# One square per score tile, or two half squares: splitting the square bank by bank

## The chip, the cores and the metric

The kernel runs on one core of one Trainium2 chip. The time is the device time of one execution in microseconds (us); medians are over all runs in the normal ("fast") state. The span of a profile leaves out the launch, so it is some 2 us shorter than the time. A trace is the profile of one execution. The engines are named as the profile names them: PE (matmuls), PEld (its weight loads), DVE, ACT, POOL (GpSimd) and SP (queue of transfers).

## The reference, cut to what matters

```python
# q, k, v: 8 batches, 12 heads, 448 positions, 64 wide
scores = scale * np.matmul(q, k.transpose(0, 1, 3, 2))
attn = np.maximum(scores, 0.0) ** 2 / S            # relu, then square
out = np.matmul(attn, v)
# then a two-layer network over 3584 tokens:
h = x @ w_in                                       # 768 -> 2048
g = np.maximum(h, 0.0) ** 2
return g @ w_out                                   # 2048 -> 768
```

The change touches one line of this: how the square in `attn` is cut into instructions.

## The kernel before

A unit is four heads of one batch. Its scores are made in tiles of two banks of PSUM, `sp[0]` and `sp[1]`, of up to 512 columns each. DVE or ACT takes the relu of each bank (from PSUM to `rel`, in fp32), and then **one** instruction on ACT or POOL squares both halves into `at` (or `comb`), which the value matmuls read:

```python
"rel": fixed(sb, "rel", 4, [P, 1024], FP32),
# ...
def square(op, sp, width, pool="at"):
    at, r = Buf(pool), Buf("rel")
    # ... rel() and dst() are views [128, 2, width] of the two buffers
    n = 2 * width
    first = [plan.add([
        dve(width, lambda e=e: nc.vector.tensor_scalar(
            out=rel()[:, e], in0=sp[e].tile[:, 0:width], ...)),        # relu and scale
        act(width, lambda e=e: nc.scalar.activation(
            out=rel()[:, e], in_=sp[e].tile[:, 0:width], func=AF.Relu, scale=SK))],
        [op], [sp[e], r], due=plan.now + 0.2) for e in range(2)]
    second = plan.add([
        act(n, lambda: nc.scalar.activation(out=dst(), in_=rel(), func=AF.Square)),
        ("POOL", 0.0018 * n + 0.05, 0.0018 * n + 0.08,
         lambda: nc.gpsimd.tensor_mul(dst(), rel(), rel()))],
        first, [r, at], due=plan.now + 4.0)
    return second, at
```

Nothing is emitted in the order of this text. `plan.add` records an operation with its alternatives (engine, price, duration), and a planner simulates the engines before the kernel is built, for 16 sets of rules (four patiences by four leads), and emits the order that ends first in its own model.

The first 21 score rounds (three units) are done in two parts: a first of 128 columns per round (`comb` tiles, 512 wide), and a later part of 320. They are "the start" below, 27 squares; the other 147 tiles are 448 wide per bank.

Of the kernel before, what the change touches and what calls it, by code (L numbers as in the profile page):

```python
# [12 lines left out]
FP32 = mybir.dt.float32  # L13
AF = mybir.ActivationFunctionType
ALU = mybir.AluOpType
# [274 lines left out]
def kernel(  # L290
# [9 lines left out]
    nc = tc.nc  # L300
# [7 lines left out]
    P = 128  # L308
# [9 lines left out]
    SK = 256.0  # L318
# [4 lines left out]
    sb = ctx.enter_context(tc.tile_pool(name="sb", bufs=1))  # L323
    psum = ctx.enter_context(tc.tile_pool(name="ps", bufs=1, space=bass.MemoryType.PSUM))

    def fixed(pool, name, n, shape, dt):
        return [pool.tile(shape, dt, name=f"{name}{i}", tag=f"{name}{i}") for i in range(n)]
# [13 lines left out]
        "rest": fixed(sb, "rest", 2, [P, NF, P], FP16),  # L341
        "comb": fixed(sb, "comb", 6, [P, NH, P], FP16),
        "part": fixed(sb, "part", 6, [P, HALF], FP32),
        "rel": fixed(sb, "rel", 4, [P, 1024], FP32),
        "mm": fixed(psum, "mm", 8, [P, 512], FP32),
    }
    plan = Plan(pools, {"PE": 5.0, "ACT": 0.7, "DVE": 1.2, "POOL": 1.4, "SP": 0.7})
    plan.cold = 6.6

    def act(n, emit):  # L350
        return "ACT", 0.09 + 0.00081 * n, 0.187 + 0.00081 * n, emit

    def dve(n, emit):
        return "DVE", 0.07 + 0.001045 * n, 0.149 + 0.001045 * n, emit
# [137 lines left out]
    def scores(rounds, bufs, cols, joint, at=None):  # L492
# [4 lines left out]
        def emit():  # L497
            for j, (n, t) in enumerate(rounds):
                qT, kT = qkt[n, "q"][1].tile, qkt[n, "k"][1].tile
                sp, c0 = bufs if joint else bufs[2 * j:2 * j + 2], j * w if joint else 0  # L500
                for e in range(2):
                    for f in range(2):
# [11 lines left out]
                       [y for x in turned for y in x[0]], bufs + [x[1] for x in turned],  # L514
                       "tile", at)

    def square(op, sp, width, pool="at"):
        at, r = Buf(pool), Buf("rel")
        flat = [2, width]

        def rel():
            return r.tile[:, 0:2 * width].rearrange("p (e c) -> p e c", e=2)

        def dst():
            t = at.tile
            if pool == "comb":
                t = t.rearrange("p f c -> p (f c)").rearrange("p (e c) -> p e c", e=2)
            return t[:, :, 0:width]

        n = 2 * width  # L530
        first = [plan.add([
            dve(width, lambda e=e: nc.vector.tensor_scalar(  # L532
                out=rel()[:, e], in0=sp[e].tile[:, 0:width], scalar1=0.0, scalar2=SK,
                op0=ALU.max, op1=ALU.mult)),
            act(width, lambda e=e: nc.scalar.activation(  # L535
                out=rel()[:, e], in_=sp[e].tile[:, 0:width], func=AF.Relu, scale=SK))],
            [op], [sp[e], r], due=plan.now + 0.2) for e in range(2)]
        second = plan.add([
            act(n, lambda: nc.scalar.activation(out=dst(), in_=rel(), func=AF.Square)),  # L539
            ("POOL", 0.0018 * n + 0.05, 0.0018 * n + 0.08,  # L540
             lambda: nc.gpsimd.tensor_mul(dst(), rel(), rel()))],  # L541
            first, [r, at], due=plan.now + 4.0)
        return second, at

    xts: dict = {}
    xt_ops: dict = {}
# [3 lines left out]
    def av(n, ts, cols=WHOLE, at=None):  # L550
        b, u = divmod(n, NU)
        x = xts.setdefault(b, Buf("xt"))
        w = cols.stop - cols.start
        first = cols == PARTS[0]
        joint = first and u > 0
        c0 = u * w if first else 0
        if ts[0] == 0:
            opened[n] = opened[n - 1] if joint else [Buf("mm"), Buf("mm")]
        banks = opened[n]
        used = [ats.pop((n, t)) for t in ts]  # L560

        def emit():
            vs = vst[n][1].tile
            for t, (_, buf, view) in zip(ts, used):
                a = view(buf.tile)
                for e in range(2):
                    for c in range(2):
                        f = c ^ e
                        r = slice(64 * c, 64 * c + 64)
                        nc.tensor.matmul(  # L570
                            banks[f].tile[64 * e:64 * e + 64, c0:c0 + w],
                            lhsT=vs[r, e ^ c, t * D:(t + 1) * D],
                            rhs=a[r, e, :],
                            start=(t == 0), stop=(t == TJ - 1), skip_group_check=True)

        before = av_ops.get(n, [])[-1:] + (av_ops[n - 1][-1:] if joint else [])
        op = plan.pe(max(0.1, 0.000437 * w) * len(ts), emit, [z[0] for z in used] + [vst[n][0]] + before,
                     [z[1] for z in used] + [vst[n][1]] + banks, "tile", at)
        av_ops.setdefault(n, []).append(op)
        if ts[-1] < TJ - 1 or (first and u < NU - 1):  # L580
            return op
        for f in range(2):
            def put(kind, f=f):
                def run():
                    dst, src = x.tile[:, 2 * u + f, cols], banks[f].tile[:, 0:w]
                    if joint:
                        dst = x.tile[:, f:NM:2, cols]
                        src = banks[f].tile[:, 0:NU * w].rearrange("p (u c) -> p u c", c=w)
                    if kind == "ACT":
                        nc.scalar.activation(out=dst, in_=src, func=AF.Copy, scale=CX)  # L590
                    else:
                        nc.vector.tensor_scalar_mul(dst, src, CX)
                return run

            n_el = NU * w if joint else w
            xt_ops.setdefault((b, cols.start), []).append(plan.add(
                [act(n_el, put("ACT")), dve(n_el, put("DVE"))], av_ops[n][-1:],
                [banks[f], x], due=plan.now + 0.2))
        return op
# [415 lines left out]
    def put(part, rs):  # L1015
        for r in rs:
            ats[r] = held.pop((part, *r))
        for n in sorted({n for n, _ in rs}):
            av(n, [t for m, t in rs if m == n], PARTS[part])
# [5 lines left out]
    def tile(part, rs, at=None):  # L1025
        cols = PARTS[part]
        w = cols.stop - cols.start
        sp = [Buf("mm"), Buf("mm")]
        op = scores(rs, sp, cols, True, at)
        second, at = square(op, sp, len(rs) * w, "at" if part else "comb")  # L1030
        for j, (n, t) in enumerate(rs):
            def view(tl, j=j, w=w, part=part):
                if not part:
                    tl = tl.rearrange("p f c -> p (f c)").rearrange("p (e c) -> p e c", e=2)
                return tl[:, :, j * w:(j + 1) * w]
            held[part, n, t] = second, at, view
# [19 lines left out]
    for z, one in enumerate(ORDER.split()):  # L1056
        at, n = 15.0 + 0.01 * z, int(one[1])
# [7 lines left out]
    for i in range(2, STREAM):  # L1065
# [3 lines left out]
        if i % TJ == 2 and i > TJ:  # L1069
            n = i // TJ - 1  # L1070
# [12 lines left out]
    for i in range(STREAM // 2, NB):  # L1083
# [19 lines left out]
        for n, t in rs:  # L1103
            sp = [Buf("mm"), Buf("mm")]
            op = scores([(n, t)], sp, WHOLE, False)
# [4 lines left out]
        for op, sp, n, t in todo:  # L1110
            second, at = square(op, sp, S)
            ats[n, t] = second, at, lambda tl: tl
        if i in avs:
            last, chain = chain, av(avs[i], list(range(TJ)))
            last.glue = chain
# [9 lines left out]
    for j in sorted(j for j in avs if j >= NB):  # L1125
        av(avs[j], list(range(TJ)))
# [35 lines left out]
```

## Time and profile before

| | before |
|---|---|
| median time (3 runs) | 383.08 us (382.96 to 383.53) |
| profiled span, granted clock | 382.0 us, 0.994 |
| busy PE / DVE / ACT / POOL | 371.8 / 268.5 / 272.0 / 191.0 us |
| squares on ACT / POOL | 110 / 64 |
| 4th first-layer group starts | 31.95 us |
| first group of the ordinary first layer starts | 35.89 us |
| PE busy between 57 and 88 us | 30.73 of 31 us |

The first layer for the three units of the start has a special form: four groups of six matmuls `mm<-w,xt`, each over one quarter of the first weight matrix. Then comes its ordinary form, `mm<-xt,w`. The profile lines themselves are in the prediction.

### The profile page before, as it was taken

How to read it: one execution, taken by the hardware profiler on the slowest of the kernel's cores; microseconds unless marked ns; L12 is line 12 of the kernel's file. 1: busy time of each engine (PE TensorE's matmuls, PEld its weight loads, DVE VectorE, ACT ScalarE, POOL GpSimd, SP SyncE). 2: the span in 40 equal slices, each digit the busy share in tenths (PEclk: the TensorE clock that was granted, in tenths of full speed). 3: DMA queues.
4: the chain of work that ended last, by engine and by line, in shares of the span. 5: the costliest groups of instructions: out<-in, count | busy, mean ns of one | idle time of the engine just before them, and what ended most of it. 6: DMA issues, size and time to landing. Idle time of an engine off the chain costs nothing.

```text
span 382.0 us, 8653 instructions
## 1 busy us (share of the span) xinstructions
PE 371.8 (97%) x3283; PEld 197.9 (52%) x3283; DVE 268.5 (70%) x464; ACT 272.0 (71%) x500; POOL 191.0 (50%) x184
## 2 busy tenths in 40 slices
PE   7799999999999999999999999999999999999995
PEld 3445565544465445544554555545555545555553
DVE  2976889687975677687996575885886768256731
ACT  4998999699877788687876786786794784244221
POOL 7987768383726665565564554664641333001000
PEclk9989999999999999999999999999999999999999
DMA  8999998987278966559369664674553002300243
GB/s 179 194 208 198 195 225 221 247 194 167 48 184 190 159 177 135 120 142 206 79 127 218 159 169 73 180 170 94 129 105 82 2 1 54 73 21 0 61 106 82
DMA packets 70216, 51.34 MB, mean 134 GB/s; under 512 B 36896, under 2 KB 70176, under 8 KB 70176
## 3 DMA queue, kind: packets, MB, share of 16 engines
q1 hardware_dynamic: 52384, 35.86, 38.2%
q0 software_dynamic: 16928, 14.09, 24.6%
q10 hardware_dynamic: 864, 0.85, 0.6%
q8 instruction: 25, 0.41, 0.4%
q14 instruction: 15, 0.12, 0.1%
HBM read 45.61 MB, written 11.01 MB: 148 GB/s over the span
## 4 chain that ended last, share of the span: by engine, by line
PE 92%; ACT 2%; DMA 2%; DVE 1%; POOL 1%; issue 1%; POOLq 0%; ACTq 0%
PE mm L632 38%; PE mm L846 31%; PE mm L505 10%; PE mm L570 8%; PE mm L781 3%; DMA g<-in_q_dram 2%; PE mm L681 2%; PE mm L444 1%; ACT comb L539 1%; DVE comb L825 1%; ACT rel L535 0%; POOL at L541 0%; DVE g L616 0%; ACT at L539 0%; PE mm L708 0%
## 5 line engine op out<-in xcount | busy, mean ns | idle before, releaser
L632 PE MATMUL mm<-xt,w 128*128 128x448 f16 (+1 forms) x768 | 149.0, 346 | 0.1
L541 POOL TENSOR_TENSOR at<-rel 128x896 f16<-128x896 f32 (+1 forms) x63 | 102.2, 1626 | 92.5 <-DVE rel L532 76.5
L616 DVE SCALAR_TENSOR_TENSOR g<-mm,g 128x448 f16<-128x448 f32 (+1 forms) x128 | 77.3, 605 | 50.4 <-ACT g L621 48.9
L632 PEld LDWEIGHTS <-w 128*128 128x128 f16 x768 | 72.3, 98 | 70.4 <-issue 11.7
L532 DVE TENSOR_SCALAR rel<-mm 128x448 f32<-128x448 f32 (+2 forms) x172 | 95.6, 596 | 15.7 <-PE mm L505 14.1
L621 ACT ACTIVATE g<-mm 128x448 f16<-128x448 f32 (+1 forms) x128 | 68.4, 539 | 47.2 <-PE mm L632 47.1
L539 ACT ACTIVATE at<-rel 128x896 f16<-128x896 f32 (+1 forms) x105 | 97.7, 948 | 1.1 <-DVE rel L532 0.6
L535 ACT ACTIVATE rel<-mm 128x448 f32<-128x448 f32 (+2 forms) x176 | 84.8, 550 | 2.9 <-PE mm L505 2.7
L846 PEld LDWEIGHTS <-comb 128*128 128x128 f16 x416 | 39.5, 98 | 30.3 <-issue 4.3
L765 ACT ACTIVATE part<-mm 128x384 f32<-128x384 f32 x45 | 22.3, 499 | 44.6 <-PE mm L846 42.3
L505 PE MATMUL mm<-qkt,qkt 64*64 64x448 f16 (+2 forms) x756 | 52.6, 340 | 1.4 <-DVE rel L532 0.3
L424 POOL CAST blk<-raw 128x896 f16<-128x896 f32 x36 | 36.5, 1024 | 23.4 <-DMA raw<-in_k_dram 11.7
L858 DVE SCALAR_TENSOR_TENSOR part<-mm,part 128x384 f32<-128x384 f32 x52 | 28.3, 554 | 24.9 <-ACT part L765 13.8
L846 PE MATMUL mm<-wt,comb 128*128 128x384 f16 x208 | 36.8, 327 | 0.2 <-DVE comb L825 0.2
L846 PE MATMUL mm<-w,comb 128*128 128x384 f16 x208 | 36.7, 327 | 0.0
L846 PEld LDWEIGHTS <-g 128*128 128x128 f16 x264 | 25.3, 98 | 19.1 <-issue 2.7
L570 PE MATMUL mm<-at,vs 64*64 64x448 f16 (+1 forms) x672 | 35.1, 344 | 0.0
L505 PEld LDWEIGHTS <-qkt 64*64 64x64 f16 x756 | 19.1, 106 | 26.2 <-issue 21.4
L474 POOL DMA_DIRECT2D vs<-in_v_dram x48 | 29.8, 631 | 4.2 <-DVE rel L532 2.0
L846 PE MATMUL mm<-w,g 128*128 128x384 f16 x176 | 31.1, 327 | 0.1
L570 PEld LDWEIGHTS <-vs 64*64 64x64 f16 x756 | 22.2, 108 | 14.7 <-issue 4.9
L747 POOL COPY rest<-g 128x1024 f16<-128x1024 f16 x8 | 8.8, 1103 | 40.6 <-DVE g L616 40.6
(61 smaller groups left out, 207.8 us busy)
## 6 DMA issues: line engine op xcount, KB each, us to landing
out_dram<-part SPq DMA_DIRECT2D x108, 96.0 KB, 2.2
raw<-in_k_dram SPq DMA_DIRECT2D x18, 448.0 KB, 4.2
raw<-in_q_dram SPq DMA_DIRECT2D x18, 448.0 KB, 5.0
vs<-in_v_dram POOLq DMA_DIRECT2D x48, 112.0 KB, 4.3
w<-in_moe_w_in_dram POOLq DMA_DIRECT2D x4, 768.0 KB, 11.8
w<-in_moe_w_out_dram POOLq DMA_DIRECT2D x4, 768.0 KB, 13.5
g<-in_k_dram POOLq DMA_DIRECT2D x4, 224.0 KB, 11.4
g<-in_q_dram POOLq DMA_DIRECT2D x4, 224.0 KB, 9.9
```

What stands on the lines that cost most here:

```text
L424: return lambda: fn(blk.tile.rearrange("p t (f d) -> p f t d", f=2), tile_of().rearrange("p f (t d) -> p f t d", d=D))
L474: nc.gpsimd.dma_start(out=buf.tile[64 * r:64 * r + 64], in_=src[:, u, hs])
L505: nc.tensor.matmul(sp[e].tile[64 * c:64 * c + 64, c0:c0 + w].rearrange("p (t c) -> p t c", c=TP), lhsT=kT[r, t, 64 * e:64 * e + 64], rhs=q ...
L532: dve(width, lambda e=e: nc.vector.tensor_scalar(out=rel()[:, e], in0=sp[e].tile[:, 0:width], scalar1=0.0, scalar2=SK, op0=ALU.max, op1=AL ...
L535: act(width, lambda e=e: nc.scalar.activation(out=rel()[:, e], in_=sp[e].tile[:, 0:width], func=AF.Relu, scale=SK))],
L539: act(n, lambda: nc.scalar.activation(out=dst(), in_=rel(), func=AF.Square)),
L541: lambda: nc.gpsimd.tensor_mul(dst(), rel(), rel()))],
L570: nc.tensor.matmul(banks[f].tile[64 * e:64 * e + 64, c0:c0 + w], lhsT=vs[r, e ^ c, t * D:(t + 1) * D], rhs=a[r, e, :], start=(t == 0), sto ...
L616: nc.vector.scalar_tensor_tensor(out=dst, in0=src, scalar=0.0, in1=dst, op0=ALU.is_gt, op1=ALU.mult)
L621: nc.scalar.activation(out=dst, in_=src, func=AF.Square)
L632: nc.tensor.matmul(bank.tile[:, c0:c0 + w], lhsT=w1[f // 4][:, m, f % 4 * P:(f % 4 + 1) * P], rhs=xts[b].tile[:, m, cols], start=(m == 0), ...
L846: nc.tensor.matmul(buf.tile[:, 0:HALF], lhsT=lhs()[:, j, :], rhs=w[:, j, :], start=(first and j == 0), stop=(j == NH - 1), skip_group_chec ...
```

## The change

Its intent: a half can be squared as soon as its own relu is done, by whichever engine is free, and its buffer comes free earlier. Relu buffers become 8 of 512 columns in place of 4 of 1024. The core of the diff (the relu itself is as before):

```diff
-        "rel": fixed(sb, "rel", 4, [P, 1024], FP32),
+        "rel": fixed(sb, "rel", 8, [P, 512], FP32),
...
+    def squared(op, bank, width, dst, at):
+        r = Buf("rel")
+        first = plan.add([dve(width, ...), act(width, ...)],
+            [op], [bank, r], due=plan.now + 0.2)
+        return plan.add([
+            act(width, lambda: nc.scalar.activation(
+                out=dst(), in_=r.tile[:, 0:width], func=AF.Square)),
+            ("POOL", 0.0018 * width + 0.05, 0.0018 * width + 0.08,
+             lambda: nc.gpsimd.tensor_mul(dst(), r.tile[:, 0:width], r.tile[:, 0:width]))],
+            [first], [r, at], due=plan.now + 4.0)
...
-        second = plan.add([... one square over 2 * width ...], first, [r, at], ...)
-        return second, at
+        return [squared(op, sp[e], width, lambda e=e: dst(e), at)
+                for e in range(2)], at
...
-        op = plan.pe(..., [z[0] for z in used] + [vst[n][0]] + before,
+        op = plan.pe(..., [y for z in used for y in z[0]] + [vst[n][0]] + before,
```

More of the change, by code (lines that the diff above doesn't have):

```diff
@@ L515, in scores, with dst @@
                        "tile", at)
-    def square(op, sp, width, pool="at"):
-        at, r = Buf(pool), Buf("rel")
-        flat = [2, width]
-        def rel():
-            return r.tile[:, 0:2 * width].rearrange("p (e c) -> p e c", e=2)
-        def dst():
+    def squared(op, bank, width, dst, at):
+        r = Buf("rel")
+        first = plan.add([
+            dve(width, lambda: nc.vector.tensor_scalar(
+                out=r.tile[:, 0:width], in0=bank.tile[:, 0:width], scalar1=0.0, scalar2=SK,
+                op0=ALU.max, op1=ALU.mult)),
+            act(width, lambda: nc.scalar.activation(
+                out=r.tile[:, 0:width], in_=bank.tile[:, 0:width], func=AF.Relu, scale=SK))],
+            [op], [bank, r], due=plan.now + 0.2)
+        return plan.add([
+            act(width, lambda: nc.scalar.activation(
+                out=dst(), in_=r.tile[:, 0:width], func=AF.Square)),
+            ("POOL", 0.0018 * width + 0.05, 0.0018 * width + 0.08,
+             lambda: nc.gpsimd.tensor_mul(dst(), r.tile[:, 0:width], r.tile[:, 0:width]))],
+            [first], [r, at], due=plan.now + 4.0)
+    def square(op, sp, width, pool="at"):
+        at = Buf(pool)
+        def dst(e):
             t = at.tile
@@ L527, in dst @@
                 t = t.rearrange("p f c -> p (f c)").rearrange("p (e c) -> p e c", e=2)
-            return t[:, :, 0:width]
-        n = 2 * width
-        first = [plan.add([
-            dve(width, lambda e=e: nc.vector.tensor_scalar(
-                out=rel()[:, e], in0=sp[e].tile[:, 0:width], scalar1=0.0, scalar2=SK,
-                op0=ALU.max, op1=ALU.mult)),
-            act(width, lambda e=e: nc.scalar.activation(
-                out=rel()[:, e], in_=sp[e].tile[:, 0:width], func=AF.Relu, scale=SK))],
-            [op], [sp[e], r], due=plan.now + 0.2) for e in range(2)]
-        second = plan.add([
-            act(n, lambda: nc.scalar.activation(out=dst(), in_=rel(), func=AF.Square)),
-            ("POOL", 0.0018 * n + 0.05, 0.0018 * n + 0.08,
-             lambda: nc.gpsimd.tensor_mul(dst(), rel(), rel()))],
-            first, [r, at], due=plan.now + 4.0)
-        return second, at
+            return t[:, e, 0:width]
+        return [squared(op, sp[e], width, lambda e=e: dst(e), at)
+                for e in range(2)], at
     xts: dict = {}
@@ L576, in av @@
         before = av_ops.get(n, [])[-1:] + (av_ops[n - 1][-1:] if joint else [])
-        op = plan.pe(max(0.1, 0.000437 * w) * len(ts), emit, [z[0] for z in used] + [vst[n][0]] + before,
+        op = plan.pe(max(0.1, 0.000437 * w) * len(ts), emit, [y for z in used for y in z[0]] + [vst[n][0]] + before,
                      [z[1] for z in used] + [vst[n][1]] + banks, "tile", at)
```

## The prediction

> **What bounds the kernel now.** I read the engine totals and the chain of work that ended last, then the busy time by stretches, then the waits.
>
> ```profile
> PE 371.8 (97%) x3283; PEld 197.9 (52%) x3283; DVE 268.5 (70%) x464; ACT 272.0 (71%) x500; POOL 191.0 (50%) x184
> ...
> PE 92%; ACT 2%; DMA 2%; DVE 1%; POOL 1%; issue 1%; POOLq 0%; ACTq 0%
> ```
>
> TensorE (PE) is busy 97% of 382 us and is 92% of the chain; the three engines that the change touches are about 4% of it, some 15 us. A busy PE need not run at its peak, so I looked for the stretch where it is starved. The columns are the stretch, its length, busy time of PE, PEld, DVE, ACT and POOL, then granted clock, DMA share and GB/s:
>
> ```profile
> 12.00:16.00 4.00, 3.08 (x83) 1.80 (x78) 3.38 (x8) 3.89 (x7) 4.00 (x5) 1.00 1.20 189
> 16.00:20.00 4.00, 2.54 (x64) 1.77 (x67) 3.74 (x10) 4.00 (x7) 4.00 (x7) 0.89 1.23 202
> 20.00:24.00 4.00, 4.00 (x46) 1.92 (x42) 3.22 (x8) 4.00 (x9) 3.98 (x4) 0.69 1.23 203
> ...
> 40.00:60.00 20.00, 19.89 (x215) 11.74 (x213) 17.38 (x35) 19.57 (x42) 14.30 (x15) 1.00 1.25 237
> ```
>
> From 12 to 20 us PE is busy 5.62 of 8 us while ACT and POOL are full: there relu and square are the limit. The low clock of the next stretch follows it. From 40 us on PE is full, with ACT close to full until 60. The waits of PE on a square (total, times, longest) are only these:
>
> ```profile
> PE mm L570 <- ACT comb L539: 1.3, 2, 0.7
> ```
>
> The starved start ends at another limit. First-layer group L681 (4 groups of 6 matmuls) needs the four quarters of the first weight matrix, and its last group starts the moment the last quarter lands; this is the timeline of weight loads:
>
> ```profile
> 31.58 0.10 PEld L991 LDWEIGHTS <-part 128*128 128x128 f16 x1
> 31.87 1.04 PEld L681 LDWEIGHTS <-xt 128*128 128x128 f16 x6 [0.19 <-DMA w<-in_moe_w_in_dram]
> ```
>
> The quarters are issued from POOL at 10.7 to 14.4 us and take up to 17.4 us to land: 14.4 + 17.4 = 31.8. The DMA share is over 1.2 all that time.
>
> [...]
>
> **The change part by part.** These groups carry the squares (busy, mean ns of one):
>
> ```profile
> L541 POOL TENSOR_TENSOR at<-rel 128x896 f16<-128x896 f32 x54 | 91.0, 1686 | 91.3 <-DVE rel L532 75.3 <-ACT rel L535 8.5 <-PE mm L570 5.3
> L539 ACT ACTIVATE at<-rel 128x896 f16<-128x896 f32 x93 | 88.9, 973 | 1.0 <-DVE rel L532 0.6 <-ACT g L621 0.2
> ...
> L541 POOL TENSOR_TENSOR at<-rel 128x640 f16<-128x640 f32 x9 | 11.2, 1263 | 1.3 <-DVE rel L532 1.2
> ...
> L539 ACT ACTIVATE at<-rel 128x640 f16<-128x640 f32 x12 | 8.8, 752 | 0.0
> ```
>
> Two sizes per engine give an estimate for a half. ACT: (973 - 752)/256 = 0.863 ns per element, fixed part 200 ns. POOL: (1686 - 1263)/256 = 1.65 ns, fixed part 206 ns. A half of 448 then costs 587 ns on ACT and 946 on POOL; 320: 476 and 735; 512: 642 and 1052; 128: 310 and 418.
>
> The built instruction lists give the counts. Relu stays the same (DVE 172 to 171, ACT 176 to 177). Of 174 squares, 110 ran on ACT and 64 on POOL; of 348 half squares ACT has 160 of 448, 24 of 320, 7 of 512 and 1 of 128; POOL has 134, 18, 3 and 1.
> - ACT: 93.9 + 11.4 + 4.5 + 0.3 = 110.1 us against 102.9 (88.9 + 8.8 + 5.2): +7 us, so 279 us, 73% of the span.
> - POOL: 126.8 + 13.2 + 3.2 + 0.4 = 143.6 us against 102.9 (91.0 + 11.2 + 0.7): +41 us, so 232 us, 61%. Share was moved to it as well as fixed parts added.
> - Both lie beside PE work wherever PE is full, so by themselves they cost nothing.
>
> What reaches the path:
> - **Start, up to the fourth L681 group: 0 us.** Both kernels put the same PE work ahead of that group (84 + 84 score, 84 + 56 value, 18 first-layer matmuls), but the changed one has 13 filler matmuls ahead of it instead of 8, six of them directly before it: its order expects to arrive early and wait. The last weight quarter is issued on POOL after the squares of one half of 512 (1.05) and one of 320 (0.74) in place of one of 640 (1.27); before, POOL also idled 0.53 us there. So its issue moves by about 0, and [...]so does its landing near 31.9 us.
> - **Order of PE after that: -0.9 us.** From there the changed list has 110 switches between the 64x64 kind (scores, values) and the 128x128 kind, not 118. In the chain a score block of 8 costs 0.50 us after dense work and 0.38 after other 64x64 work; an 8-matmul dense block 1.41 against 1.30. A pair costs 0.12 + 0.11 = 0.23; four pairs 0.9. From about 88 us the two orders are the same.
> - **A bank wait at 57.2 us: -0.3 us.** The chain has 0.55 us of ACT relu between two score blocks there. The blocks are reordered around it; I count half of it as gained.
> - **POOL running late before 40 us: +0.4 us.** Counted from the lists, POOL does 12.0 us of squares before it issues the loads of k and q for unit 5 (34.2 us), and in the changed one about 16.8. It had 3.2 us idle between 26 and 33 us to take that in, so the issue slips by about 1.6 us. They took 5.6 and 5.9 us to land, at about 39.8 and 40.9, and PE used them at 41.3. So PE could wait up to about 1.2 us; I take a third.
>
> Sum: 0 - 0.9 - 0.3 + 0.4 = -0.8 us, so 382.3 us.
>
> **The rivals.**
> - *The start gets shorter.* PE idles 2.4 us between 12 and 20 us, the first L681 group took 1.92 us where later ones took 1.29 (0.6, the clock), and smaller waits make another 1 us: 4 us at most, 379 us. For it: full ACT and POOL there, and halves that can start before their partner's relu. Against it: the landing of the weights at 31.87 us, and ACT's total before the last first-part square falls only by 1.4 us by my count while POOL gets three squares of 1.05 us there.
> - *POOL becomes the bound.* It takes 41 us more, and also issues the value and weight loads and casts k and q. For it: the order gives POOL 134 halves in rows of up to ten. Against it: POOL waited 91 us for its input before, and 61% leaves room. If values wait for it regularly, 1 to 4 us more: 384 to 387.
> - *ACT becomes the bound until 60 us.* It was busy 19.57 of 20 us there and gets a fixed part of 200 ns more often; back-to-back operations overlap, and POOL takes more of the squares. It would cost 1 us: 384.
>
> **Range and chances.** The pinned landing makes a large gain unlikely, and a PE-bound middle makes a large loss unlikely. I predict 382.3 us, range 380.6 to 384.4. Over 2% faster (under 375.4) needs 7.7 us, more than the 4 us that the start could give: 0.01. Over 2% slower (over 390.7) needs POOL or ACT to hold PE through the middle: 0.03. Within 2%: 0.96.
>
> **What would show it.** Right: the fourth first-layer group again waits for the weights near 31.9 us, after a longer wait with fillers; ACT near 279 and POOL near 232 us busy; a POOL half of 448 near 0.95 us and an ACT half near 0.59; PE waits after 88 us no longer than before. Wrong on the start: that group begins well before 31 us. Wrong on POOL: PE waits on POOL squares, or on the k and q of unit 5 at 41 us by more than 1.2 us. Wrong on the switches: the stretch from 32 to 88 us is not shorter.

Two passages that no trace of this case shows are cut from this text and marked. No term of the sum is among them: it came to 0 - 0.9 - 0.3 + 0.4 = -0.8 us, as it stands. The ground for "so does its landing", that the DMA was saturated, was not shown (the page of the kernel before has 221 to 247 GB/s in its slices from 48 to 76 us, against 189 to 203 between 12 and 24 us), and the step is the author's estimate. So is "by themselves they cost nothing", which the runs below test. Two statements have their numbers elsewhere in the same trace: a busy PE need not run at its peak (20 to 24 us: busy 4.00 of 4.00 us at a granted clock of 0.69), and ACT's back-to-back operations overlap (93 squares of 973 ns are 90.5 us, their group is busy 88.9).

## More of the kernel before

An engine that comes free takes the most urgent operation it can do:

```python
def pick(self, eng, now, waiting):
    for z, (_, _, op) in enumerate(waiting):
        # ...
            if len(alt) == 5 and eng == "POOL" and sum(x > now for x in self.sent) > 7:
                continue            # POOL issues no load while over 7 are open
        # ...
```

So a change of any price or size can change the whole order of the program. The order also fixes what stands behind what on POOL, which issues the loads of values and weights itself, between its squares.

## The result, and the profile after

| | before | after |
|---|---|---|
| median time (4 runs each, same job) | 383.15 us | 385.94 us (384.86 to 386.11) |
| ratio, 95% interval | 1 | 1.0066 (1.0046 to 1.0086) |
| profiled span | 382.0 us | 384.2 us |
| 4th first-layer group starts | 31.95 us | 32.02 us |
| first ordinary first-layer group starts | 35.89 us | 37.03 us |
| PE busy, 57 to 88 us | 30.73 us | 29.73 us |

A ratio here is the mean time of one kernel's fast runs over the mean of the other's fast runs of the same rounds, so it is not quite the ratio of the medians quoted. The changed kernel is within 2%, but it is slower by some 2.5 us and lies above the predicted range.

Two cautions about size first. A trace is one execution; whole executions of the kernel before scatter over some 2 us (its spans in one later job ran from 380.3 to 382.6), so a difference of 2.2 us between two traces is read by *where* it arises rather than by its last decimal. And but for fillers (matmuls of no use, which the planner emits where it has no other work for PE) the two have the same matmul work: whatever PE spends longer on, it waited for, or paid for in the order, in fillers or in a lower clock.

From the page of the changed kernel, engine totals and the chain of work that ended last:

```profile
PE 373.1 (97%) x3288; PEld 199.4 (52%) x3288; DVE 270.2 (70%) x461; ACT 271.3 (71%) x585; POOL 229.2 (60%) x276
...
PE 88%; DVE 5%; POOL 3%; ACT 2%; issue 1%; DVEq 0%; ACTq 0%; POOLq 0%
```

PE still bounds the kernel, and POOL took 38 us more. But DVE and POOL are now 8% of the chain where they were 2%. The squares by shape (busy in us, mean ns of one):

```profile
L531 POOL TENSOR_TENSOR at<-rel 128x448 f16<-128x448 f32 x134 | 125.7, 958 | 74.6 <-DVE rel L521 61.5 <-ACT rel L524 12.1 <-PE mm L571 0.9
...
L528 ACT ACTIVATE at<-rel 128x448 f16<-128x448 f32 x160 | 87.7, 601 | 1.4 <-DVE rel L521 0.8 <-PE mm L571 0.5
```

The single durations are those predicted (946 and 587 ns). Note the ACT row: 160 x 601 ns is 96.2 us, but the group is busy 87.7 us. Back-to-back instructions of ACT overlap, and busy time counts the overlap once; so mean durations must not be multiplied into a busy time.

The stretches of the start, changed kernel (busy of PE, PEld, DVE, ACT, POOL, then the granted clock):

```profile
12.00:16.00 4.00, 2.20 (x76) 1.43 (x75) 2.97 (x6) 3.94 (x10) 4.00 (x6) 1.00 1.24 196
16.00:20.00 4.00, 3.54 (x74) 2.36 (x73) 3.69 (x9) 3.44 (x10) 3.98 (x6) 0.66 1.24 202
20.00:24.00 4.00, 3.70 (x51) 1.97 (x49) 3.75 (x10) 3.81 (x12) 3.98 (x7) 0.92 1.23 203
```

PE is as starved as before, 5.74 of the 8 us to 20, only earlier; and the low clock follows the starved stretch again, one stretch earlier (0.66 after 2.20 of 4 us busy; before, 0.69 after 2.54). The first first-layer group does start earlier (20.20 us, before 21.42), but 0.27 us of that lead are left at the second group (24.29, before 24.56), and the fourth starts at 32.02 us against 31.95: nothing is left of it. The two fourth groups start at the same time for different reasons. Before, PE waited for the last weight quarter, which landed at 31.8 us (issued at 14.4, 17.4 to land). In the changed kernel it landed at 31.1 us (14.1 and 17.0), 0.9 us before the group starts:

```profile
L479 POOL DMA_DIRECT2D w<-in_moe_w_in_dram x4: 826/862/888, 10.8 to 14.1; - x4
DMA to landing us min/median/max: 8.4/12.1/17.0
```

What stood in front of the group were five fillers, which themselves waited for DVE:

```profile
31.38 0.81 PE L992 MATMUL mm<-part 128*128 128x256 f16 x5 [0.39 <-DVE comb L690]
32.02 1.46 PE L682 MATMUL mm<-w,xt 128*128 128x512 f16 x6
```

**The first place that loses: 33 to 37 us.** POOL in the changed kernel, in order of time (start, length, engine, line, what; in brackets the idle time ahead and what ended it):

```profile
29.65 0.66 POOL L474 DMA_DIRECT2D vs<-in_v_dram  x1
31.58 0.59 POOL L474 DMA_DIRECT2D vs<-in_v_dram  x1 [1.27 <-DMA w<-in_moe_w_in_dram]
32.19 3.42 POOL L531 TENSOR_TENSOR at<-rel 128x320 f16<-128x320 f32 x5
```

and in the kernel before:

```profile
29.71 0.66 POOL L474 DMA_DIRECT2D vs<-in_v_dram  x1
32.37 0.59 POOL L474 DMA_DIRECT2D vs<-in_v_dram  x1 [2.00 <-DVE rel L532]
32.98 1.27 POOL L541 TENSOR_TENSOR at<-rel 128x640 f16<-128x640 f32 x1
```

A load of values comes in two issues. In both kernels the second is held for 1.3 to 2.0 us, until 0.5 us after the last weight quarter has landed. Before, one whole square stood behind it; now five half squares do, and they are done at 35.6 us. The values that need them wait. PE of the changed kernel:

```profile
33.92 0.74 PE L571 MATMUL mm<-at,vs 64*64 64x320 f16 x16
34.99 0.46 PE L571 MATMUL mm<-at,vs 64*64 64x320 f16 x6 [0.33 <-POOL at L531]
35.67 0.46 PE L571 MATMUL mm<-at,vs 64*64 64x320 f16 x6 [0.22 <-POOL at L531]
```

and of the kernel before:

```profile
33.84 1.15 PE L570 MATMUL mm<-at,vs 64*64 64x320 f16 x28
```

The same 28 matmuls, followed in both by the same transposes, take 2.14 us from first start to next block (33.92 to 36.06) instead of 1.08 (33.84 to 34.92): **+1.06 us**, nearly all of the 1.14 by which the ordinary first layer starts later.

**The second place: 57 to 88 us.** The stretch in the changed kernel, then before:

```profile
57.00:88.00 31.00, 29.73 (x280) 15.96 (x279) 26.68 (x41) 27.09 (x61) 24.22 (x30) 1.00 1.00 214
```

```profile
57.00:88.00 31.00, 30.73 (x284) 15.40 (x277) 24.94 (x40) 27.57 (x49) 20.63 (x21) 1.00 0.98 217
```

One whole microsecond of PE is lost. The timeline of PE and PEld in the changed kernel shows most of it as one wait:

```profile
76.15 0.38 PE L505 MATMUL mm<-qkt,qkt 64*64 64x448 f16 x4
...
77.36 0.14 PEld L505 LDWEIGHTS <-qkt 64*64 64x64 f16 x4 [1.10 <-DMA qkt<-blk]
77.39 0.38 PE L505 MATMUL mm<-qkt,qkt 64*64 64x448 f16 x4 [0.86 <-DVE w L811]
```

Read by PE's own line, DVE's combination of weights (L811) held it. Read with the line of PEld above it, the truth is another: the weight load of the same matmul waited 1.10 us for a transposing transfer of q or k (`qkt<-blk`), and the matmul starts 0.03 us behind that weight load. (In the trace of e15, below, the same piece of DVE work stands at the same distance, and these scores do not wait for it.) That transfer was issued on SP at 70.57 us, behind an issue that had begun at 68.64. The rest of the microsecond is small: the changed order puts 16 score matmuls directly ahead of the values of the same tiles, with no dense block in between, and PE waits 0.15 and 0.24 us for relu at these two seams.

**A third place, near 197 us.** Comparing fixed stretches hides what a new order gains, and what it loses where PE counts as busy. So compare the times at which PE has done the same number of matmuls of every kind, fillers aside (counted in the traces; the first column is the start of the next block in the kernel before, the others say how much later that point comes; e15, e3 and c1 are runs described below):

| before | after | e15 | e3 | c1 |
|---|---|---|---|---|
| 31.95 us | +0.07 | -0.16 | -0.57 | -0.53 |
| 34.92 us | +1.14 | -0.15 | -0.57 | +0.66 |
| 58.09 us | +0.88 | -0.41 | -0.67 | +1.15 |
| 101.46 us | +1.81 | -0.53 | -0.23 | +1.20 |
| 195.77 us | +2.45 | +0.11 | +0.41 | +1.12 |
| 376.29 us | +2.22 | -0.11 | +0.25 | +1.84 |

The changed kernel loses 1.07 us at the first place, gets 0.26 back before 58 us, loses 0.93 around the second, and another 0.64 between 101 and 196 us. There one block of eight scores is stretched, in the kernel before and in the changed one:

```profile
195.25 0.58 PE L505 MATMUL mm<-qkt,qkt 64*64 64x448 f16 x8
```

```profile
197.00 1.28 PE L505 MATMUL mm<-qkt,qkt 64*64 64x448 f16 x8
```

Its last pair waits for relus of ACT, which ACT began only at 196.89 us, behind two half squares and another operation. That block takes 1.28 us in the trace of each of the nine kernels in which the later tiles are split and planned anew (the changed one, e3, e4, e9 to e13, e15), and 0.55 to 0.58 us in those of all the others. So these 0.7 us go with halves, or with the order that the planner gives to halves; no run here separates the two.

### The profile page after: what moved, and what is told of

Its sections match the earlier page's. It is cut to its first block, busy times and chain, and to the rows that moved or that the text cites. A ratio compares the mean times of both kernels' runs of the same rounds, so it can differ in the third digit from the quotient of the medians.

```text
span 384.2 us, 8786 instructions
## 1 busy us (share of the span) xinstructions
PE 373.1 (97%) x3288; PEld 199.4 (52%) x3288; DVE 270.2 (70%) x461; ACT 271.3 (71%) x585; POOL 229.2 (60%) x276
## 4 chain that ended last, share of the span: by engine, by line
PE 88%; DVE 5%; POOL 3%; ACT 2%; issue 1%; DVEq 0%; ACTq 0%; POOLq 0%
PE mm L633 37%; PE mm L847 29%; PE mm L505 9%; PE mm L571 8%; PE mm L782 3%; DVE comb L826 1%; DVE rel L521 1%; POOL at L531 1%; PE mm L444 1%; PE mm L989 1%; ACT at L528 1%; POOL w L479 1%; POOL comb L531 1%; DVE part L859 1%; DVE w L811 0%
## 5 line engine op out<-in xcount | busy, mean ns | idle before, releaser
L531 POOL TENSOR_TENSOR at<-rel 128x448 f16<-128x448 f32 (+1 forms) x152 | 138.2, 930 | 74.7 <-DVE rel L521 61.5
L521 DVE TENSOR_SCALAR rel<-mm 128x448 f32<-128x448 f32 (+3 forms) x171 | 95.3, 594 | 18.8 <-PE mm L505 16.1
L528 ACT ACTIVATE at<-rel 128x448 f16<-128x448 f32 (+1 forms) x184 | 97.5, 584 | 1.4 <-DVE rel L521 0.8
L424 POOL CAST blk<-raw 128x896 f16<-128x896 f32 x36 | 35.4, 995 | 12.8 <-DMA raw<-in_k_dram 5.4
L571 PE MATMUL mm<-at,vs 64*64 64x448 f16 (+1 forms) x672 | 36.5, 344 | 0.9 <-POOL at L531 0.5
L571 PEld LDWEIGHTS <-vs 64*64 64x64 f16 x756 | 23.0, 109 | 15.5 <-issue 4.9
L748 POOL COPY rest<-g 128x1024 f16<-128x1024 f16 x8 | 9.7, 1216 | 34.4 <-DVE g L617 34.4
```

Of the source, the lines that this page charges most:

```text
L424: return lambda: fn(blk.tile.rearrange("p t (f d) -> p f t d", f=2), tile_of().rearrange("p f (t d) -> p f t d", d=D))
L521: dve(width, lambda: nc.vector.tensor_scalar(out=r.tile[:, 0:width], in0=bank.tile[:, 0:width], scalar1=0.0, scalar2=SK, op0=ALU.max, op1= ...
L528: act(width, lambda: nc.scalar.activation(out=dst(), in_=r.tile[:, 0:width], func=AF.Square)),
L531: lambda: nc.gpsimd.tensor_mul(dst(), r.tile[:, 0:width], r.tile[:, 0:width]))],
L571: nc.tensor.matmul(banks[f].tile[64 * e:64 * e + 64, c0:c0 + w], lhsT=vs[r, e ^ c, t * D:(t + 1) * D], rhs=a[r, e, :], start=(t == 0), sto ...
```

## The experiments

Eighteen kernels ran. All gave correct results except one. Medians of the kernel before in the same jobs were 383.1 to 383.6 us; the ratio of each run is to these. The theories at first: (H) the fixed parts of the added instructions cost time where ACT is full; (O) the planner's new order costs it; (B) the smaller buffers do; (P) POOL became the bound.

### Halves in place, the order untouched

**e1_two_halves_in_place.** The kernel before, with each square emitted as two instructions, one after the other, on the engine that had it. Order, engines and buffers are those of before; PE and DVE have the same instruction lists.

```diff
-            act(n, lambda: nc.scalar.activation(out=dst(), in_=rel(), func=AF.Square)),
+            act(n, lambda: [nc.scalar.activation(out=dst()[:, e], in_=rel()[:, e], func=AF.Square) for e in range(2)]),
...
-             lambda: nc.gpsimd.tensor_mul(dst(), rel(), rel()))],
+             lambda: [nc.gpsimd.tensor_mul(dst()[:, e], rel()[:, e], rel()[:, e]) for e in range(2)])],
```

> The order, the engines and the buffers of the kernel before, but each square is issued as two halves on the engine that had it (174 more instructions, no other difference). Theory A (the fixed parts of the added instructions make the squares late): +1 to +2.5 us, 384.2 to 385.7, with POOL near 225 us busy and PE waiting on POOL squares. Theory B (the new order and the new sharing between ACT and POOL, not the added instructions, cost the time): within 0.5 us of before, about 383.2, though POOL's busy time rises nearly as much.

Measured: 386.96 us, ratio 1.0089 (1.006 to 1.0117). So the mere presence of the extra instructions, gaining nothing from them, costs 3.4 us. Its engine totals:

```profile
PE 372.5 (97%) x3283; PEld 196.9 (51%) x3283; DVE 268.0 (70%) x464; ACT 280.5 (73%) x610; POOL 200.7 (52%) x248
```

ACT has 110 instructions more and is busy 8.5 us longer, 77 ns each; POOL 64 more and 9.7 us, 151 ns each. The ordinary first layer starts at 37.87 us, 1.98 later than before; the profiled span is 2.8 longer.

**e5_in_place_start_only.** The same, but only the 27 squares of the start are emitted in two.

```diff
+    ... [two halves] if width != S else [the whole square] ...       # in both alternatives of e1
```

> As the two halves in place (order, engines, buffers of before; +3.4 us), but only the 27 squares of the start (512 and 320 wide) are issued as two. In the trace of that run PE had lost 1.8 us more than before by 36 us and 2.8 us in all. Theory A1 (added fixed parts cost where ACT and POOL are full, in the start): +1.8 to +2.2 us, 385.1. Theory A2 (they cost evenly, a little at each of the 174 squares): 27 of 174, so +0.5 us, 383.6.

Measured: 385.55 us, ratio 1.0047 (0.9996 to 1.0099), scattering over 2 us (384.49 to 386.43). The interval touches 1, but its trace shows the mechanism. Stretches (columns as above) and first-layer groups on PE:

```profile
16.00:20.00 4.00, 2.24 (x49) 1.09 (x49) 3.58 (x9) 4.00 (x10) 4.00 (x8) 0.90 1.22 197
20.00:24.00 4.00, 4.00 (x39) 2.10 (x39) 3.31 (x8) 4.00 (x13) 3.98 (x7) 0.50 1.23 204
24.00:28.00 4.00, 4.00 (x45) 1.66 (x42) 1.27 (x3) 2.50 (x8) 3.11 (x5) 0.75 1.25 207
```

```profile
22.14 2.74 PE L681 MATMUL mm<-w,xt 128*128 128x512 f16 x6
24.81 1.70 PE L570 MATMUL mm<-at,vs 64*64 64x320 f16 x28
...
34.21 0.27 PE L991 MATMUL mm<-part 128*128 128x256 f16 x1 [0.51 <-ACT xt L590]
34.31 1.46 PE L681 MATMUL mm<-w,xt 128*128 128x512 f16 x6
```

The fourth first-layer group starts at 34.31 us, 2.36 later than before, in three terms. The first group starts 0.72 late (22.14, before 21.42): ACT is full, and its added instructions delay PE (e6, below, has them alone). Then the group takes 2.74 us (before 1.99) and the values after it 1.70 (before 1.15), together 1.30 us: the granted clock is 0.50, then 0.75, where before had 0.69, then 1.00, after a stretch in which PE was busy 2.24 us (before 2.54). The last 0.3 us is the longer wait for ACT ahead of the fourth group (0.51, before 0.19). So the added work (17 instructions of ACT, 10 of POOL; 1.3 and 1.5 us by e1's figures) delays PE by more than ACT's part of it, and **the largest term in this trace is the clock**. The trace of e1 has the same three terms: 0.92, 0.7 and 0.3. That the clock falls because the stretch before is more starved is not shown. Here are the stretches of c1, a run described below, with as little PE and the full clock after it:

```profile
16.00:20.00 4.00, 2.23 (x56) 1.42 (x55) 3.01 (x6) 4.00 (x10) 3.98 (x7) 1.00 1.22 199
20.00:24.00 4.00, 3.09 (x47) 1.78 (x48) 3.51 (x10) 4.00 (x11) 3.98 (x4) 1.00 1.25 207
```

And e15, which has the changed kernel's order on PE and is as starved from 12 to 16 us (2.23, against 2.20), is granted 1.00 in the next stretch, where the changed kernel had 0.66. The traced run of e5 was also the slowest of its four. So the clock's term can't be credited to the edit on this evidence.

**e6_in_place_act_only** and **e7_in_place_pool_only.** Only the ACT line of e1, or only the POOL line.

> Two halves in place only for the 110 squares on ACT; those on POOL stay whole. If ACT is what binds in the start (full from 12 to 32 us, and its squares are what values wait for): most of the +3.4 us, 385.5 to 386.5. If POOL is: near 383.2.

> Two halves in place only for the 64 squares on POOL; those on ACT stay whole. If ACT binds: 383.0 to 383.5, as before. If POOL binds (its queue also carries the loads): +1.5 us or more.

Measured: 385.46 us, ratio 1.0063 (1.0017 to 1.0109), for ACT; 383.75 us, 1.0021 (0.9969 to 1.0072), for POOL. The added instructions of ACT, which in the trace of before is busy 19.4 of the 20 us from 12 to 32 us, cost; those of POOL can't be told from nothing. The traces say the same of the start: the fourth first-layer group begins at 33.06 us with ACT's halves (1.11 late) and at 32.02 with POOL's (0.07 late). In the trace of e6 the first group runs at full length (1.47 us), so these 1.11 us are ACT's delay without a loss of clock in that group. Later, PE waits 0.56 us for DVE at 90 us in the traces of e1 and e6, and not in those of before, e5 and e7: in these two traces halves of the later tiles on ACT are not free either.

### Halves in one stage only, planned anew

In these the planner sees the halves as separate operations and may order them, as in the changed kernel, but both halves lie in one old buffer of 1024 columns, of which there are 4:

```diff
+        if split:                      # set for tiles of the start, for later tiles, or for both
+            return [plan.add([act(width, ...square of half e...), ("POOL", ...)],
+                [first[e]], [r, at], due=plan.now + 4.0) for e in range(2)], at
         second = plan.add([...the whole square...])
-        return second, at
+        return [second], at
```

**e2_split_start_only.** Split for the start only.

> The split only in the first stage (units 0 to 2, tiles of 512 and 320), with whole buffers; whole squares later. In the changed kernel PE lost 1.1 us to late POOL squares at 34 to 36 us and another 1.1 us or so between 57 and 200 us. If the start loss belongs to the split of the start: about +1.1 us, 384.3, with PE waiting on POOL squares near 35 us. If it came only from how the order fell: 383 to 383.5.

Measured: 390.23 us, ratio 1.018 (1.0135 to 1.0225). This run was confounded: in the new order the planner gave two pieces of the combination of second-layer weights to POOL, 3.1 us each, and PE waited 3.9 us for one transposing transfer.

**e8_split_start_combine_dve.** The same with the POOL alternative of that combination taken out, so that DVE does all of it, as in the kernel before.

```diff
-                plan.add([("POOL", 3.06, 3.1, ...nc.gpsimd.tensor_sub...),
-                          ("DVE", 0.9, 0.98,
+                plan.add([("DVE", 0.9, 0.98,
```

> The split only in the first stage again (+7.1 us in the first try), but the weight combination may run on DVE only, as it does in before; in the first try the scheduler put two pieces of 3.1 us on POOL, and PE waited 3.9 us for a transposed k or q behind them. If that choice made the loss: 383.5 to 384.5, the rest being the start. If the split of the start itself costs more: above 386.

Measured: 386.43 us, ratio 1.0079 (1.0033 to 1.0124). So 3.8 of the 7 us of e2 went with that choice of the planner, which has nothing to do with halves; splitting the start itself still came with +3 us.

**e3_split_later_only.** Split for the later tiles only; up to about 32 us PE has the same list as before.

> The split only after the first stage (tiles of 448), with whole buffers. Theory A and B both: the start is that of before, so no loss at 34 to 36 us; what is lost between 57 and 200 us (about 1.1 us net of the gain of fewer switches) stays: 384.2. If the later split is harmless: 382.3 to 383.2, since it has 126 switches between matmul kinds in place of 134 (0.9 us).

Measured: 383.76 us, ratio 1.0014 (0.9995 to 1.0033). 294 halves instead of 147 squares, where the bulk of them is: no gain, and no cost that can be told from zero (the interval allows up to 1.3 us). In its trace the start is 0.57 us ahead, by chance, as PE's list there is that of before, and the end 0.25 behind: the later part has lost 0.8 us, 0.64 of it at the third place. Theory (P) falls with it: POOL is busy 227.5 us here, as in the changed kernel (229.2), and the time stays.

**e4_split_old_buffers.** Split everywhere, in the old buffers.

> The split everywhere, but both halves of a tile stay in one buffer of 1024 (four of them, as before) that comes free after the second square. If the sharing of halves is the cause: as the changed kernel, 385 to 386. If the half-size buffers are the cause: near 383. If the half buffers help: above 386.

Measured: 385.87 us, ratio 1.0072 (1.0048 to 1.0096), like the changed kernel (1.0066). So the loss needs no half-size buffers, and theory (B) is not needed. That the buffers neither help nor hurt is not shown: the planner gave another order, and in this trace PE waited 2.2 us for the first weight quarter, so the fourth first-layer group is 1.96 us late (0.07 in the changed kernel). The totals agree, the places do not.

### Controls: other orders, with and without halves

If a new order alone can cost 2.5 us, then (O) needs no halves. So I changed one number of the planner and ran whole squares and halves under the same rule.

**c1_before_other_order.** The kernel before, whole squares, with POOL's price for a square set to what the trace shows (206 ns + 1.65 ns per element). That gives another order: 38 squares of 896 on POOL instead of 54.

```diff
-            ("POOL", 0.0018 * n + 0.05, 0.0018 * n + 0.08,
+            ("POOL", 0.00165 * n + 0.157, 0.00165 * n + 0.206,
```

> A control for what an order is worth: the kernel before, whole squares, with the same new price formula, which for whole squares changes little (1.635 for 1.663 us) but tips the scheduler to another order (128 switches for 134, 38 squares of 896 on POOL for 54). If orders as such differ by 1 to 3 us: 384 to 386, and losses of this size in the changed kernel need no cause in the halves. If not: 382.5 to 383.5.

**e11_true_pool_price.** The changed kernel with that formula.

> The changed kernel with the price of a half square on POOL in the scheduler set to what the trace shows (0.157 us + 1.65 ns per element between starts, in place of 0.05 + 1.8 ns, which was right for whole squares of 896 and is 0.04 to 0.06 us short for halves). If the loss comes from a scheduler that takes POOL's halves for cheaper than they are: 383 to 384.5. If not: 385 to 387.

Measured: c1 385.42 us, ratio 1.006 (1.0042 to 1.0077); e11 384.96, 1.0048 (1.0028 to 1.0068). This is the control that weighs most: **whole squares in another order lose 2.2 us**, about what the changed kernel loses. It waits in the same two stretches (values for a POOL square, 0.65 us, ordinary first layer at 36.55 us; PE busy 29.98 us between 57 and 88), but by the table of equal work the second costs it next to nothing (1.15 to 1.20), and it loses 0.7 us after 196 us instead. Its order also gives POOL one piece of the weight combination (3.1 us at 58 us), as in e2. And c1's first first-layer group starts at 20.17 us, as early as the changed kernel's 20.20, so even that earlier start can't be credited to the halves.

**e9_one_load_fewer**, **c2_before_one_load_fewer**, **c3_before_two_loads_fewer** and **e12_two_loads_fewer.** POOL's limit on open loads is lowered from 7 to 6 or 5, aimed at the held load of 31 us; e9 and e12 are the changed kernel, c2 and c3 the kernel before.

```diff
-                if len(alt) == 5 and eng == "POOL" and sum(x > now for x in self.sent) > 7:
+                if len(alt) == 5 and eng == "POOL" and sum(x > now for x in self.sent) > 6:    # or > 5
```

> The changed kernel, but the scheduler keeps one load fewer open from POOL (7, not 8). In the changed kernel a value load held POOL for 1.27 us at 30.3 us until the last weight quarter landed, and five half squares stood behind it, which values waited for (1.1 us by 36 us). Here no square stands behind that load. If the held load is the cause of that 1.1 us: the first 448-column layer group (37.0 us, 35.9 in before) starts near 36, and the time falls by about 1 us to 385. If POOL is simply too full: no change.

> Whole squares with the scheduler rule of the run with one load fewer (half squares, 385.5 us): its partner. If another order as such costs about 2 us at the start: 384.5 to 387, no better than its partner with halves. If whole squares are better than halves under equal rules: 383 to 383.5.

> Whole squares with two loads fewer open (limit 6). The same reading: 384.5 to 388 if the order as such costs; near 383 if halves cost.

> Half squares with two loads fewer open, the partner of the run before it. If halves cost nothing of their own once the order differs anyway: within 1 us of the partner. If halves cost the 2.5 us that the changed kernel lost: 2 us or more above it.

| planner's rule | whole squares | halves |
|---|---|---|
| as given | 383.15 | 385.94 |
| true price of POOL (c1, e11) | 385.42 | 384.96 |
| one load fewer (c2, e9) | 390.03 | 385.46 |
| two loads fewer (c3, e12) | 384.68 | 388.27 |

Ratios to before: c2 1.0184, e9 1.0058, c3 1.0032, e12 1.014; e9 scatters from 383.59 to 387.17. Halves are slower in two rows, faster in one, and level within the intervals in one. Under whole squares alone the rule moves the time by almost 7 us. So the sign of "halves against wholes" over the whole kernel is not a property of the halves here (the 0.7 us of the third place may be); the order of before is simply the best of all the orders tried, and anything that moves it is likely to lose.

**e10_last_start_tiles_on_act.** The changed kernel, with POOL barred from the squares of the last tiles of the start.

```diff
-        tile(1, rounds[i:i + 1])
+        tile(1, rounds[i:i + 1], None, i < 15)          # False: squares of this tile on ACT only
```

> The changed kernel, but the squares of the last six tiles of the start (rounds 15 to 20) may not go to POOL; ACT was busy only 2.35 of 4 us from 32 to 36 us. If late POOL squares cost the 1.1 us there: about 385 and PE no longer waits on POOL squares at 35 us. If ACT is what binds: no gain, or worse.

Measured: 385.51 us, ratio 1.0064 (1.0046 to 1.0082). PE no longer waits for a POOL square there: the values run in one piece (34.37 us, 1.25 long). The ordinary first layer still starts at 36.93 us, but more other work lies ahead of it; at equal work, its second group, PE is only 0.22 us later than before (37.85 against 37.63), where the changed kernel is 1.14 later. So the wait at 34 us went, as in e15, and the time hardly fell: this order loses 1.65 us between 101 and 196 us, 0.7 of it at the third place.

**e13_later_only_true_price.** e3 with the true price, the best case I could think of for halves.

> Whole squares and the order of before up to 32 us, halves only later, with the measured price of a half on POOL. The run with the old price gave +0.5 us (383.8). If the halves can give anything where PE is full: below 382.5. If they are worth nothing there: 383 to 384.

Measured: 384.69 us, ratio 1.0037 (1.001 to 1.0064). Nothing gained.

### Two tests of single causes

**e14_start_act_squares_halved.** Wrong results (relative error 0.14): the kernel before, in which ACT squares only half of the columns of each first-part tile, so ACT has some 2.1 us less to do while it is full (an estimate from two traces: five squares, of 1056 ns for 1024 columns in the kernel before and 628 ns for 512 in the changed one). The other columns are zeroed at the outset.

```diff
-            act(n, lambda: nc.scalar.activation(out=dst(), in_=rel(), func=AF.Square)),
+            act(n, lambda: nc.scalar.activation(out=dst()[:, :, 0:width // 2], in_=rel()[:, :, 0:width // 2], func=AF.Square)
+                if pool == "comb" else nc.scalar.activation(out=dst(), in_=rel(), func=AF.Square)),
```

> Wrong results on purpose: order, engines and buffers of before, but the five squares of 1024 that ACT does in the start cover only half of their columns (the rest is zeroed by DVE in its idle time before 4 us), so ACT is relieved of about 5 x 0.43 = 2.1 us where it is full. If the weights, landing at 31.9 us, pin the end of the start as the prediction said: the fourth first-layer group still starts at 31.4 to 31.9, and the time falls by less than 0.7 us. If only ACT binds there: that group starts near 30, and the time falls by 1.5 to 2.1 us.

Measured: 382.72 us, ratio 0.9984 (0.996 to 1.0008). This is what such a relief brings: 2.1 us of ACT taken away gives 0.4 us or nothing. In the timeline of its profiled run, the fourth first-layer group starts when POOL's held load is released, at 31 us:

```profile
30.98 0.59 POOL L474 DMA_DIRECT2D vs<-in_v_dram  x1 [1.57 <-PE mm L505]
30.99 1.46 PE L681 MATMUL mm<-w,xt 128*128 128x512 f16 x6
```

The first group starts 0.73 us earlier than before (20.69), the fourth 0.96 (30.99), at neither of the times expected. The last weight quarter went out earlier too, POOL having issued three quarters from 12.00 us, and it had landed by 30.5 us (13.7 and 16.8); what PE waited for just before the group was ACT (0.19 us). So this trace does not show the weights as the limit, and how the start moves with them stays open. Work taken off ACT gains less than half of itself here (0.96 of 2.1 us); work added cost most of itself in e6 (1.11 of 1.3).

**e15_load_after_squares.** The changed kernel in which only the held value load is moved, behind the five half squares that it held up. All else keeps its order.

```diff
+        i = [position of the value load of unit 4 in self.order]
+        j = [position of the 5th POOL square after it]
+        self.order.insert(j + 1, self.order[i])
+        del self.order[i]
         for emit in self.order:
```

> The changed kernel with one move in its POOL queue: the value load of unit 4 is issued after the five half squares that stood behind it, everything else in the same order on every engine. In the changed kernel that load held POOL from 30.3 to 31.6 us and PE then waited for those squares. If that is the 1.1 us lost by 36 us: the first 448-by-320 layer group starts near 36.0 us instead of 37.0 and the time falls by about 1 us, to 384.9. If PE would have waited there for ACT or DVE anyway: 385.9 again.

Measured: 385.39 us, ratio 1.0052 (1.0025 to 1.0079); the runs are 383.92 (profiled), 386.02, 385.49, 385.49, 385.3 and 384.94. In its profiled run the first two losing places are gone, and the third is not. PE:

```profile
33.69 1.15 PE L579 MATMUL mm<-at,vs 64*64 64x320 f16 x28
```

```profile
57.00:88.00 31.00, 30.59 (x282) 16.47 (x275) 26.89 (x40) 28.03 (x63) 26.14 (x30) 1.00 1.04 201
```

The values run in one piece, the ordinary first layer starts at 35.74 us, and in the later stretch the scores no longer wait for a transposing transfer, though PE's order there is the same as in the changed kernel. Its span, 381.9 us, equals that of before. But that execution was the fastest of its six, by 1.0 us or more; the median is only 0.5 us below the changed kernel's, and the intervals overlap. So the hold is the cause of the wait at 34 us (take it away, and the wait goes), but how much of the usual time it is worth, between 0 and about 1 us, is not settled. Nor is why the transposing transfer came in time: it was issued 1.8 us earlier, with PE 1.3 us earlier.

No version beat the kernel before: none with correct results had a median below its 383.1.

## Why the prediction was right or wrong

- **PE as the bound: right. "Start, up to the fourth L681 group: 0 us": the number right (0.07), the reason not, and so in part luck.** The weights were to hold that group again "near 31.9 us"; they landed at 31.1, and fillers and a wait for DVE stood in front of it. In e1, e5 and e6 it starts 1.1 to 2.4 us late, over 1 us after the last quarter has landed.
- **Durations and POOL: right.** 958 and 601 ns for a half of 448, POOL busy 229 us (predicted 232). ACT is 271, not 279: the sum multiplied single durations, which overlap in busy time (160 of 601 ns are 96.2 us, and the group is busy 87.7).
- **"POOL running late before 40 us: +0.4 us": the failing step on this side.** The slip of the loads of k and q for unit 5 was sized well (issue at 35.57 us against 34.18, so 1.4; predicted 1.6), but they cost nothing: PE transposed them at 42.44 us with no wait. What paid was the value matmuls of the start, behind five half squares that were themselves behind a held load: +1.06 us in the trace. I had counted how much work stands ahead of the loads, and not what stands behind them.
- **"A bank wait at 57.2 us: -0.3 us": right.** By the table of equal work PE gains 0.26 us between 35 and 58 us, in the changed kernel and in e15.
- **"Order of PE after that: -0.9 us": the failing step on the other side.** Between 58 and 101 us PE lost 0.93 us instead: one transposed q or k came 0.9 us too late in that trace, and PE, with scores directly ahead of their own values, waits for relu (0.15 and 0.24 us). Without the late transfer (e15) the gain there is 0.12 us, not 0.9. And "from about 88 us the two orders are the same" is wrong: they differ until about 200 us, and lose 0.64 us on the way, which undoes what e15 had gained.
- **The sum.** In the trace, 0.07 + 1.07 - 0.26 + 0.93 + 0.64 - 0.23 (after 196 us) makes 2.2 us, where the prediction had -0.8. The timed runs put it at 2.5 (ratio 1.0066).
- **"Both lie beside PE work wherever PE is full, so by themselves they cost nothing": true only with its condition.** In the start PE is not full and ACT is (5.62 and 7.89 of the 8 us from 12 to 20 us, before). There the fixed parts alone, with the order held, delay the ordinary first layer by 2.0 to 2.4 us (e1, e5), a third to a half of it through a lower granted clock in those traces, and by 1.11 with ACT's alone and no such loss in the first group (e6). In the later tiles the timed runs show no cost that can be told from zero (e3), but the traces show the 0.7 us of the third place. That the changed kernel pays this cost is not shown: it gave part of the squares to POOL, and its fourth group is on time.
- **The range.** It was built from the terms above as if a new order were a known quantity. c1 shows that a new order with no halves in it moves this kernel by 2.2 us, c2 by almost 7. A range from 380.6 to 384.4 had no room for that.
- **The rivals.** "The start gets shorter" was right for the first group (1.2 us), but most of it was gone by the second group, and not through the landing of the weights, as argued against it. "POOL becomes the bound ... 384 to 387" has the right number and the wrong reason: POOL is 60% busy, and its squares held PE for 0.8 us in one wait and 0.5 us in two more together.

What stays open: how the usual 2.5 us divide between the three places and the rest of the order, since one trace is one execution; whether the third place comes with halves in any order; and what makes most executions of e15 over 1 us longer than its traced one.

## What to carry to other kernels

In the start, where ACT was full, the fixed parts of its added instructions (17, an estimated 1.3 us by e1's 77 ns each) set the fourth first-layer group back by 1.11 us (e6); POOL's 10 (1.5 us by e1's 151 ns) set it back by 0.07 (e7). Where a cut does pay was not found here, since no version gained. A low clock in one trace (0.50 in e5) may be chance: look for as starved a stretch without it (1.00 in c1, after 2.23 of 4 us busy) before you give it a cause. When a tuned schedule is planned anew, treat the new order as an uncertainty of 1% in its own right (with whole squares, c1 lost 0.6% and c2 1.8%), run a control that changes the order, and compare traces at points of equal work. A milestone that stays on time does not show that the same thing holds it. Behind a load issue on POOL that may be held, put nothing that somebody needs soon (1.27 us of idle POOL and 1.06 us of PE in the trace of the changed kernel); and when a matmul's wait names an engine, look at its weight load too before believing it (at 77.36 us it had waited 1.10 us, for a transfer).
